# A planned mixer kernel: whole loads, low-rank matrices loaded earlier, halved weight casts, and ring space in the plan's queue model

## The chip, the cores and the metric

One core of one Trainium2 chip. The metric is the device time of one execution in microseconds (us). The kernel before takes 176.11 us (median of three runs, 175.78 to 177.19).

## The reference

A gated linear recurrence over 4 batches of 8 heads, 768 steps and 48 features, then a mixer: a low-rank mix along the sequence (U is 768 x 32, V is 32 x 768), and a two-layer MLP along the model dimension (384 to 1536 to 384, relu) with residuals.

```python
for t in range(S):
    state = alpha[:, :, t, :, None] * state + np.einsum('bhd,bhe->bhde', k[:, :, t], v[:, :, t])
    y[:, :, t] = np.einsum('bhd,bhde->bhe', q[:, :, t], state)
x = y.transpose(0, 2, 1, 3).reshape(B, S, H * D)
u = x + (x.transpose(0, 2, 1) @ U @ V).transpose(0, 2, 1)
out = u + np.maximum(u @ w_ch1, 0.0) @ w_ch2
```

## The kernel before

The kernel is written as a list of operations, each with an engine, an assumed cost, what it reads and writes, and a priority. When the kernel is built, a small planner (`Plan.run`) simulates the engines with these costs and fixes **the order of the instructions on every engine**. On the chip each engine takes its instructions in that fixed order and waits on semaphores. So an assumed cost takes no time itself.

All transfers go through one queue, SyncE's. Its model in the planner:

```python
if eng == "SP":
    clock[eng] = max(t + op.hold, dma)          # an issue waits for the transfers before it
    dma = max(dma, t + 1200.0) + op.cost        # a load is given 4400 ns
    op.end = dma + 1700.0                       # data there 1700 ns later
```

The loads of a batch, those of the last one in pieces of 4, 2, 3 and 8 heads:

```python
cuts = (4, 2, 3, 8)
def pieces(t, src, n):
    w = cuts[n] if b in (3,) else H
    for h0 in range(0, H, w):
        h1 = min(h0 + w, H)
        nc.sync.dma_start(t()[:, h0 * NC : h1 * NC, 0:D], src[b, h0:h1].rearrange("h (c p) d -> p (h c) d", p=C))
for n, (t, src) in enumerate(zip(ts, (alpha, k, q, v))):
    P.add("SP", 4400, lambda t=t, src=src, n=n: pieces(t, src, n), w=[t], prio=b + n / 10)
```

For each group of two chunks of 128 steps (three groups a batch), the kernel makes rk and rq (k and q times the decay factors) and rv (v cast to bf16), transposes rk and rq into kt and qt (by TensorE in batches 0 and 1, by the DMA in batches 2 and 3), multiplies them to scores, masks these (pm), and forms the state and y. Then come the low-rank mix (utx, xb), its transposed form uT, and the MLP. The sizes of buffers and the engine of each copy are tables. Where TensorE has nothing to do early on, the planner inserts filler products, meant to keep its clock up.

Of the kernel before, what the change touches and what calls it, by code (L numbers as in the profile page):

```python
# [48 lines left out]

class Op:  # L50
    __slots__ = ("eng", "cost", "fn", "prio", "deps", "bufs", "n", "end", "users", "est", "i", "hold")


class Plan:
# [12 lines left out]
    def add(self, eng, cost, fn, r=(), w=(), prio=0.0, after=(), kind=None, hold=450.0):  # L67
        op = Op()
        op.eng, op.cost, op.fn, op.prio = eng, cost, fn, prio
        op.i, op.hold = len(self.ops), hold  # L70
        op.deps, op.users, op.est, op.end = set(), [], 0.0, None
        for k in r:
            d = self.writer.get(k)
            if d is not None:
                op.deps.add(d)
        for k in w:
            d = self.writer.get(k)
            if d is not None:
                op.deps.add(d)
            op.deps.update(self.readers.get(k, ()))  # L80
        for k in r:
            self.readers.setdefault(k, []).append(op)
        for k in w:
            self.writer[k] = op
            self.readers[k] = []
        op.deps.update(x for x in after if x is not None)
        if kind is not None:
            if kind in self.kinds:
                op.deps.add(self.kinds[kind])
            self.kinds[kind] = op  # L90
        op.deps.discard(op)
        op.bufs = []
        for k in list(r) + list(w):
            b = k[0] if isinstance(k, tuple) else k
            if isinstance(b, Buf) and b not in op.bufs:
                op.bufs.append(b)
        for b in op.bufs:
            b.left += 1
        self.ops.append(op)
        return op  # L100

    def run(self):
# [10 lines left out]
        dma = 0.0  # L113
        fill = self.fill[0]
        todo = len(self.ops)
        while todo:
# [42 lines left out]
            if eng == "SP":  # L159
                clock[eng] = max(t + op.hold, dma)  # L160
                dma = max(dma, t + 1200.0) + op.cost
                op.end = dma + 1700.0
            else:
                clock[eng] = t + op.cost
                op.end = t + op.cost
# [26 lines left out]
def kernel(  # L192
# [12 lines left out]
    nc = tc.nc  # L205
# [39 lines left out]
    rk_s = slots("rk", 3, [C, G, H, 64], BF16)  # L245
# [11 lines left out]
    pms = Pool(slots("pm", 5, [C, 2, HP, C], BF16))  # L257
# [36 lines left out]
    def load_low_rank():  # L294
        UE, VE = ("DVE","POOL")
# [8 lines left out]
        P.add("SP", 500, lambda: nc.sync.dma_start(u_in(), moe_U.rearrange("(c p) r -> p c r", p=128)), w=[(t, 4)], prio=0.3)  # L304
        for g in range(4):
            P.add("SP", 400, lambda g=g: nc.sync.dma_start(vm_in()[32 * g : 32 * g + R, :], moe_V), w=[(t, g)], prio=0.3)
# [3 lines left out]
    def load_big():  # L310
# [4 lines left out]
        engs = ["POOL"]*6  # L315
        cost = {"ACT": 1480, "POOL": 1470}
        for i, (src, dst) in enumerate(parts):
# [7 lines left out]
            P.add("SP", 2000, lambda src=src, stage=stage: nc.sync.dma_start(stage(), src), w=[(t, i)], prio=0.5 if i < 3 else 1.35)  # L325
            P.add(engs[i], cost[engs[i]], lambda dst=dst, stage=stage, e=engs[i]: copy(e, dst, stage()), r=[(t, i)], w=[("w1" if i < 3 else "w2", i % 3)], prio=400 + i)
# [6 lines left out]
    dbank = [gen,gen3,gen3,gen3]  # L333

    def load(b):
        ts = [Buf(io) for _ in range(4)]
        cuts = (4, 2, 3, 8)

        def pieces(t, src, n):
            w = cuts[n] if b in (3,) else H  # L340
            for h0 in range(0, H, w):
                h1 = min(h0 + w, H)
                nc.sync.dma_start(t()[:, h0 * NC : h1 * NC, 0:D], src[b, h0:h1].rearrange("h (c p) d -> p (h c) d", p=C))  # L343

        for n, (t, src) in enumerate(zip(ts, (alpha, k, q, v))):
            P.add("SP", 4400, lambda t=t, src=src, n=n: pieces(t, src, n), w=[t], prio=b + n / 10)
        return ts

    def stage_gla(b, g, sprev, xb, ins):
# [8 lines left out]
        ek = ("POOL", "POOL", "DVE")[g] if first else "POOL"  # L358
        ekt = ("DVE", "DVE", "ACT")[g] if first else "ACT"
        pe = 900 + g if first else pr + 2  # L360
        eq = ("POOL", "DVE", "DVE")[g] if first else ("DVE" if b in (0,1) else "POOL")
        ev = ("POOL", "DVE", "DVE")[g] if first else "POOL"
        eqt = ("ACT", "DVE", "ACT")[g] if first else ("ACT" if b in () else "DVE")
# [4 lines left out]
        def ch(t):  # L368
            return t().rearrange("p (h c) w -> p c h w", c=NC)[:, c0 : c0 + G, :, 0:D]

        lt = Buf(lts)
        P.add("ACT", 850, lambda: nc.scalar.activation(lt()[:, :, :, 0:D], ch(at), AF.Ln), r=[at], w=[lt], prio=890 if first else pr + 4)  # L372
        rv = Buf(rvs)
        P.add(ev, ccpy[ev], lambda: copy(ev, rv(), ch(vt)), r=[vt], w=[rv], prio=pr + 3)
# [25 lines left out]
        def f_mul(eng, dst, src, fac):  # L400
            ENG[eng].tensor_tensor(dst()[:, :, :, 0:D], ch(src), fac().rearrange("t g (h d) -> t g h d", d=D), op=ALU.mult)  # L401

        P.add(ek, cmul[ek], lambda: f_mul(ek, rk, kt, ai), r=[kt, ai], w=[rk], prio=pr + 2)
        P.add(eq, cmul[eq], lambda: f_mul(eq, rq, qt, aa), r=[qt, aa], w=[rq], prio=pr + 2)

        def f_tr(src, tb):
            t = bf(tb()).rearrange("p (e c) -> p e c", c=C)
            for i in range(G):
# [8 lines left out]
        for src, dst, eng, cost in ((rk, kT, ekt, 1015 if ekt == "ACT" else 640), (rq, qT, eqt, 1015 if eqt == "ACT" else 640)):  # L417
            if b in (2,3):
                P.add("SP", 1000, lambda src=src, dst=dst: nc.sync.dma_start_transpose(dst().rearrange("p g e c -> p (g e) c"), src().rearrange("t g h w -> t (g h w)")), r=[src], w=[dst], prio=pr / 1000 - 1, hold=1250.0)  # L419
                continue  # L420
            tb = Buf(gen)
            P.add("PE", mm(*[C] * 8), lambda src=src, tb=tb: f_tr(src, tb), r=[src], w=[tb], prio=pr + 2, after=[done.get(kk - win)])
            P.add(eng, cost, lambda dst=dst, tb=tb, eng=eng: copy(eng, dst().rearrange("p g e c -> p (g e c)"), bf(tb())), r=[tb], w=[dst], prio=pr + 1)

        pm = []
        for i in range(G):
# [16 lines left out]
            P.add("PE", mm(*[C] * 4) * 1.2, f_sc, r=[kT, qT], w=[sc], prio=pr + 1, after=[done.get(kk - win)])  # L443
# [39 lines left out]
        dops[kk] = P.add("PE", mm(*[D] * 8) if final else mm(*[2 * D] * 8, *[D] * 8), f_d, r=[rk, rv], w=[db], prio=pr + 1, after=[dops.get(kk - 1), done.get(kk - 1)])  # L483
# [11 lines left out]
        em = ("ACT", "ACT", "DVE")[g] if first else "ACT"  # L495
# [25 lines left out]
        for i in range(G):  # L521
            ys.append(P.add("PE", 240, lambda i=i: f_y(i, False), r=[pm[i], rv], w=[(yb, i, 0)], prio=pr + 0.5, after=[dops[kk]]))
            sin = (sprev, 1) if i == 0 else (st, 0)
            if sin[0] is not None:
                ys.append(P.add("PE", 210, lambda i=i: f_y(i, True), r=[qT, sin], w=[(yb, i, 1)], prio=pr, after=[dops[kk]]))
# [7 lines left out]
        if b < 1 and c0 + G == NC:  # L533
# [7 lines left out]
    def stage_mix(b, xb, uT):  # L541
# [12 lines left out]
        if b < 1:  # L554
# [5 lines left out]
        P.add("ACT", 490, lambda: nc.scalar.copy(utx(), xu()[:, 0, 0:DM]), r=[(xu, 0)], w=[utx], prio=pr)  # L560
        if b == 0:
            P.fill_end = op
        if b in (0,):
            for hf in range(2):
                for j in range(NCT):
# [7 lines left out]
                    P.add("PE", mm(TW), lambda hf=hf, j=j, tb=tb: nc.tensor.matmul(tb()[:, 0, 0:TW], lhsT=utx()[:, j * C : (j + 1) * C], rhs=vm_sb[:, hf * TW : (hf + 1) * TW], start=False, stop=True, skip_group_check=True), r=[utx, "vm"], w=[tb], prio=pr)  # L573
# [3 lines left out]
        for c in range(NC):  # L577
            hb = Buf(mlp)
            P.add("PE", mm(DM), lambda c=c, hb=hb: nc.tensor.matmul(hb()[:, 0, 0:DM], lhsT=vm_sb[:, c * C : (c + 1) * C], rhs=utx(), start=True, stop=True), r=[utx, "vm"], w=[hb], prio=pr + 1)  # L579
            P.add("DVE", 550, lambda c=c, hb=hb: nc.vector.tensor_tensor(xb()[:, c, :], xb()[:, c, :], hb()[:, 0, 0:DM], op=ALU.add), r=[hb, (xb, c)], w=[(xb, c)], prio=pr)  # L580
            if b in (2,3):
                if c % 3 == 2:
                    P.add("SP", 1100, lambda c=c: nc.sync.dma_start_transpose(uT()[:, c - 2 : c + 1].rearrange("p c j t -> p (c j) t"), xb()[:, c - 2 : c + 1, :].rearrange("p c m -> p (c m)")), r=[(xb, c - i) for i in range(3)], w=[(uT, c // 3, j) for j in range(NCT)], prio=pr / 1000 - 1, hold=1300.0)
# [19 lines left out]
    def mlp1(b, uT, h1, tt):  # L603
        for jt in range(NJ):
# [13 lines left out]
            for cts in ([(0,), (1,), (2,)] if b in (0,) and jt < 2 else [(0, 1, 2)]):  # L618
                P.add("PE", mm(*[TW] * len(cts)), lambda f=f, cts=cts: f(cts), r=[n for n in need if len(n) < 3 or n[2] in cts] + [("w1", jt // 4)], w=[hb], prio=pr)
# [5 lines left out]
    def mlp2(b, xb, h1, c, utx):  # L625
        hb = Buf(mlps[b])
        pr = 5000 + b * 1000 + 100 + (c % 3) * 33 + (0 if c < 3 else 100)
        for g in range(NJ // 1):
# [8 lines left out]
            P.add("PE", mm(*[DM] * 1), f, r=[(h1, jt) for jt in range(1 * g, 1 * (g + 1))] + [("w2", g * 1 // 4)], w=[hb], prio=pr + g)  # L637
        if utx is not None:
            P.add("PE", mm(DM), lambda: nc.tensor.matmul(hb()[:, 0, 0:DM], lhsT=vm_sb[:, c * C : (c + 1) * C], rhs=utx(), start=False, stop=True), r=[utx], w=[hb], prio=pr + 9)
        ou = Buf(outs)  # L640
        P.add("DVE", 550, lambda: nc.vector.tensor_tensor(ou(), xb()[:, c, :], hb()[:, 0, 0:DM], op=ALU.add), r=[hb, (xb, c)], w=[ou], prio=100)  # L641
        P.add("SP", 550, lambda: nc.sync.dma_start(out[b, c * C : (c + 1) * C, :], ou()), r=[ou], prio=-1)
# [48 lines left out]
```

## Time and profile before

| quantity | before |
|---|---|
| median | 176.11 us |
| span of the profiled run, mean granted clock | 174.7 us, 0.990 |
| PE (TensorE) busy | 160.1 us, 92% |
| filler products within that | 16.8 us |
| first product of the MLP | 32.04 us |
| DMA packets, of them under 512 B | 63394, 37520 |
| the chain that ended last | PE 43%, DMA 24%, the queue of SyncE (SPq) 18% |

SyncE issues the transfers one after the other; as I read the traces, an issue lasts until there is room for it (0.7 us where it passes at once). The timeline of that queue gives start, duration, line, what is transferred.

```profile
11.73 4.00 SPq L343 DMA_DIRECT2D io<-in_v_dram  x1
15.78 4.45 SPq L304 DMA_DIRECT2D io<-in_moe_U_dram  x1
20.28 1.93 SPq L306 DMA_DIRECT2D io<-in_moe_V_dram  x4
```

The small U (98 kB) is issued at 15.78 us and holds the queue for 4.45 us. It has little to transfer, so what it waits for is, as I read it, v in front of it (v landed at 21.6 us).

### The profile page before, as it was taken

To read this page: it belongs to the slowest core of one execution; us is meant where nothing else is said; L and a number is where in the kernel's file an instruction comes from. 1 tells how busy PE (TensorE), PEld (TensorE's weight loads), DVE (VectorE), ACT (ScalarE), POOL (GpSimd) and SP (SyncE) were. 2 spreads that over 40 slices of the span, in tenths; PEclk is the share of its full clock that TensorE was granted. 3 is DMA by queue.
4 is the path that set the end of the run, shared out by engine and by line. 5 is a ranking of instruction groups with operands and counts; after the bars stand their busy time and mean duration, and the time that the engine had idled before them with its cause. 6 is when DMAs were issued, how large, how long until landed. Compare 5 with 4: busy or idle time off the path is not lost.

```text
span 174.7 us, 4027 instructions
## 1 busy us (share of the span) xinstructions
PE 160.1 (92%) x1696; PEld 103.0 (59%) x1696; DVE 89.9 (51%) x144; ACT 77.7 (44%) x136; POOL 53.0 (30%) x49
## 2 busy tenths in 40 slices
PE   5998798999889899989999999299999999999992
PEld 4876576666566476555665655156666566666660
DVE  1005893553695425375855738036775584543421
ACT  2284486668914391774435285205513410523200
POOL 4007378503365803796000037393000000000000
PEclk9999999999999999999999999969999999999999
DMA  3889989899989699799899989599500119101122
GB/s 94 254 246 270 258 257 388 247 269 272 266 283 378 193 276 267 228 282 200 187 245 195 238 215 256 131 201 241 120 33 16 49 50 220 45 0 49 51 85 90
DMA packets 63394, 33.39 MB, mean 191 GB/s; under 512 B 37520, under 2 KB 62096, under 8 KB 63376
## 3 DMA queue, kind: packets, MB, share of 16 engines
q1 hardware_dynamic: 63376, 33.13, 71.1%
q8 instruction: 13, 0.21, 0.5%
q14 instruction: 5, 0.04, 0.1%
HBM read 24.08 MB, written 4.72 MB: 165 GB/s over the span
## 4 chain that ended last, share of the span: by engine, by line
PE 43%; DMA 24%; SPq 18%; POOL 6%; DVE 4%; ACT 2%; issue 2%; ACTq 0%; POOLq 0%
PE ps L632 19%; PE ps L610 15%; SPq L343 12%; DMA io<-in_v_dram 9%; DMA io<-in_k_dram 6%; DMA io<-in_moe_w_ch_dram 5%; DMA io<-in_alpha_dram 4%; SPq L325 3%; SPq L419 3%; POOL rk L401 2%; PE ps L436 2%; POOL rv L292 2%; PE ps L410 1%; DVE rq L401 1%; PE ps L515 1%
## 5 line engine op out<-in xcount | busy, mean ns | idle before, releaser
L632 PE MATMUL ps<-w_sb,h1t 128*128 128x384 bf16 x288 | 57.1, 332 | 0.5 <-POOL w_sb L292 0.5
L610 PE MATMUL ps<-uT,w_sb 128*128 128x384 bf16 x288 | 52.8, 328 | 0.0
L621 ACT ACTIVATE h1t<-ps 128x384 bf16<-128x384 f32 x48 | 23.5, 490 | 44.4 <-PE ps L610 44.2
L623 DVE TENSOR_SCALAR h1t<-ps 128x384 bf16<-128x384 f32 x48 | 26.6, 556 | 24.4 <-PE ps L610 22.0
L632 PEld LDWEIGHTS <-h1t 128*128 128x128 bf16 x288 | 27.2, 99 | 18.6 <-issue 1.9
L610 PEld LDWEIGHTS <-w_sb 128*128 128x128 bf16 x288 | 27.5, 99 | 18.1 <-issue 0.8
L401 POOL TENSOR_TENSOR rk<-io,ai 128x768 bf16<-128x768 f32 x11 | 18.8, 1711 | 45.8 <-ACT ai L394 30.9
L446 DVE TENSOR_TENSOR pm<-ps,ut_ones 128x1024 bf16<-128x1024 f32 x21 | 25.4, 1221 | 8.9 <-PE ps L436 8.6
L641 DVE TENSOR_TENSOR ou<-xb,ps 128x384 f32<-128x384 bf16 x24 | 13.3, 552 | 15.7 <-PE ps L632 12.8
L645 PE MATMUL ps<-ones,ident 128*128 128x256 bf16 x122 | 16.8, 290 | 1.9 <-POOL ident masks.py:199 1.9
L531 ACT CAST xb<-ps 128x768 bf16<-128x768 f32 (+1 forms) x13 | 9.7, 749 | 12.3 <-PE ps L515 11.0
L645 PEld LDWEIGHTS <-ident 128*128 128x128 bf16 x122 | 12.2, 104 | 4.5 <-POOL ident masks.py:199 1.9
L372 ACT ACTIVATE lt<-io 128x768 bf16<-128x768 f32 x12 | 10.1, 850 | 8.3 <-DMA io<-in_alpha_dram 7.7
L401 POOL TENSOR_TENSOR rq<-io,aa 128x768 bf16<-128x768 f32 x7 | 11.5, 1641 | 4.9 <-DMA io<-in_q_dram 4.9
L292 POOL CAST rv<-io 128x768 bf16<-128x768 f32 x10 | 8.0, 824 | 10.7 <-DMA io<-in_v_dram 7.0
L580 DVE TENSOR_TENSOR xb<-xb,ps 128x384 bf16<-128x384 bf16 x18 | 9.5, 551 | 2.9 <-PE ps L579 2.6
L394 ACT ACTIVATE ai<-ps 128x768 bf16<-128x768 f32 x12 | 9.8, 819 | 2.1 <-PE ps L381 2.1
L436 PE MATMUL ps<-qt,kt 48*128 48x128 bf16 x192 | 9.2, 218 | 0.9 <-ACT xb L531 0.5
L395 ACT ACTIVATE aa<-ps 128x768 bf16<-128x768 f32 x12 | 9.9, 825 | 0.0
L292 POOL CAST w_sb<-io 128x1536 bf16<-128x1536 f32 x6 | 8.8, 1465 | 3.0 <-DMA io<-in_moe_w_ch_dram 3.0
L515 PEld LDWEIGHTS <-pm 128*128 128x128 bf16 x192 | 7.5, 96 | 2.8 <-issue 0.3
L515 PE MATMUL ps<-rv,pm 128*128 128x48 bf16 x192 | 8.4, 184 | 0.3 <-DVE pm L446 0.3
(63 smaller groups left out, 125.4 us busy)
## 6 DMA issues: line engine op xcount, KB each, us to landing
io<-in_moe_w_ch_dram SPq DMA_DIRECT2D x6, 768.0 KB, 7.7
out_dram<-ou SPq DMA_DIRECT2D x24, 192.0 KB, 2.3
io<-in_alpha_dram SPq DMA_DIRECT2D x2, 576.0 KB, 5.8
io<-in_k_dram SPq DMA_DIRECT2D x4, 288.0 KB, 4.3
io<-in_q_dram SPq DMA_DIRECT2D x2, 432.0 KB, 5.5
io<-in_moe_V_dram SPq DMA_DIRECT2D x4, 96.0 KB, 2.3
io<-in_q_dram SPq DMA_DIRECT2D x1, 288.0 KB, 6.0
io<-in_moe_U_dram SPq DMA_DIRECT2D x1, 96.0 KB, 6.3
```

The lines of the kernel that those rows point to most:

```text
L292: ENG[eng].tensor_copy(dst, src)
L343: nc.sync.dma_start(t()[:, h0 * NC : h1 * NC, 0:D], src[b, h0:h1].rearrange("h (c p) d -> p (h c) d", p=C))
L401: ENG[eng].tensor_tensor(dst()[:, :, :, 0:D], ch(src), fac().rearrange("t g (h d) -> t g h d", d=D), op=ALU.mult)
L436: nc.tensor.matmul(s2[:, par, p, :], lhsT=kT()[o : o + D, i, p, :], rhs=qT()[o : o + D, i, p, :], start=(p == 0), stop=(p == HP - 1),)
L446: nc.vector.tensor_tensor(pmi().rearrange("t two hp c -> t (two hp) c"), sc().rearrange("p two (hp c) -> p (two hp) c", c=C), maskc.to_bro ...
L515: nc.tensor.matmul(y2[:, par, p, :], lhsT=pm[i]()[:, par, p, :], rhs=rv()[:, i, 2 * p + par, :], start=s0, stop=s1, skip_group_check=True,)
L610: nc.tensor.matmul(hb()[:, 0, 0:TW], lhsT=w1_sb[:, ct, jt * 128 : (jt + 1) * 128], rhs=uT()[:, 3 * tt : 3 * tt + 3, ct, :], start=(ct == 0 ...
L621: P.add("ACT", 500, lambda jt=jt, hb=hb: nc.scalar.activation(h1()[:, jt, :], hb()[:, 0, 0:TW], AF.Relu), r=[hb], w=[(h1, jt)], prio=100)
L623: P.add("DVE", 560, lambda jt=jt, hb=hb: nc.vector.tensor_scalar_max(h1()[:, jt, :], hb()[:, 0, 0:TW], 0.0), r=[hb], w=[(h1, jt)], prio=100)
L632: nc.tensor.matmul(hb()[:, 0, 0:DM], lhsT=h1()[:, jt, (c % 3) * C : (c % 3 + 1) * C], rhs=w2_sb[:, jt, :], start=(jt == 0), stop=(jt == NJ ...
L641: P.add("DVE", 550, lambda: nc.vector.tensor_tensor(ou(), xb()[:, c, :], hb()[:, 0, 0:DM], op=ALU.add), r=[hb, (xb, c)], w=[ou], prio=100)
L645: P.fill_fn = lambda i: nc.tensor.matmul(ps[:, i, 0:256], lhsT=ident, rhs=fill_in, start=True, stop=True)
```

## The change

Its intent: load every batch whole, bring U and V in earlier (U between alpha and k, V between q and v), shorten the copies on the way to the first product of the MLP, cast the weights in halves, so that products can start after half a cast, and give the planner a queue model with 512 ring places, in which a load takes 385 places and a small transfer 40.

```diff
             if eng == "SP":
-                clock[eng] = max(t + op.hold, dma)
-                dma = max(dma, t + 1200.0) + op.cost
-                op.end = dma + 1700.0
+                free = t
+                for s, f, n in ring:
+                    x = sum(m for s2, f2, m in ring if s2 >= s) + op.descs - RING
+                    if x > 0:
+                        free = max(free, s + (f - s) * min(1.0, x / n))
+                clock[eng] = free + op.hold
+                s = max(dma, clock[eng] + 850.0)
+                dma = s + op.cost
+                ring.append((s, dma, op.descs))
+                del ring[:-24]
+                op.end = dma + op.land                 # land: 550 ns
 # low rank: U, then V
-        UE, VE = ("DVE","POOL")
+        UE, VE = ("DVE","DVE")
-        P.add("SP", 500, ... moe_U ..., prio=0.3)
+        P.add("SP", 400, ... moe_U ..., prio=0.05)
-            P.add("SP", 400, ... moe_V ..., prio=0.3)
+            P.add("SP", 300, ... moe_V ..., prio=0.205)
 # weights: each cast in two halves, those of w2 shared by POOL and ACT
-            P.add(engs[i], cost[engs[i]], ... copy(e, dst, stage()) ...)
+            for hf in range(2):
+                e = ((("POOL","POOL"),)+(("POOL","POOL"),)*2+(("POOL","ACT"),)*3)[i][hf]
+                ...
 # loads
-            P.add("SP", 4400, ... pieces(t, src, n), w=[t], prio=b + n / 10)
+            P.add("SP", 4100, ... src[b] whole ..., prio=b + n / 10, hold=800.0, descs=385)
 # engines, first batch (three groups) and others
-        ek = ("POOL", "POOL", "DVE")[g] if first else "POOL"
+        ek = ("DVE", "POOL", "DVE")[g] if first else "POOL"
-        eq = ("POOL", "DVE", "DVE")[g] if first else ("DVE" if b in (0,1) else "POOL")
+        eq = ("POOL", "DVE", "DVE+POOL")[g] if first else ("DVE" if b in (0,) else "POOL")
 # ... likewise for rv, kt, qt, st; rk 3 -> 4 buffers, pm 5 -> 4, any PSUM bank for the state;
# state product of a group allowed earlier; last group's y and its low-rank product in two steps in batches 1 and 2 too;
 # the evacuation of utx in batch 0 is split between DVE and ACT
```

The `...` stand for cuts. The arithmetic is the same.

## The prediction

> **What bounds the kernel now.** I read the page's slices first, to see which resource is full when; then the same quantities in short stretches around the one visible hole; then the queue's own order of time, to see what the hole waited for; then the DMA counts of single stretches, to see what a load costs in each form.
>
> The slices (4.37 us each):
>
> ```profile
> PE   5998798999889899989999999299999999999992
> PEclk9999999999999999999999999969999999999999
> DMA  3889989899989699799899989599500119101122
> ```
>
> Three stretches can be seen. Up to slice 28 (about 124 us) the DMA row is nearly full. PE is full too, but its first 32 us are mostly filler (L645, 16.8 us of PE's 160.1): the first product of the MLP (L610) starts at 32.04 us. From about 113 us on PE works without a gap until 171.3 us, while DMA is almost idle. Between them lies slice 25 with PE at 2, and slice 26 with the granted clock at 6. In stretches of 2 us:
>
> ```profile
> 106.00:108.00 2.00, 2.00 (x14) 1.21 (x13) 1.90 (x5) 0.53 (x1) 2.00 (x2) 1.00 1.03 298
> 108.00:110.00 2.00, 1.51 (x10) 0.79 (x8) 0.57 (x2) 1.36 (x2) 0.00 (x0) 1.00 0.62 175
> 110.00:112.00 2.00, 0.00 (x0) 0.00 (x0) 0.00 (x0) 0.15 (x1) 0.00 (x0) 1.00 0.36 117
> 112.00:114.00 2.00, 1.01 (x20) 0.78 (x20) 0.42 (x2) 0.03 (x1) 1.89 (x2) 1.00 0.92 198
> 114.00:116.00 2.00, 2.00 (x9) 0.95 (x7) 0.40 (x1) 0.28 (x1) 2.00 (x3) 0.58 1.07 243
> 116.00:118.00 2.00, 2.00 (x8) 1.01 (x7) 0.56 (x1) 0.13 (x1) 2.00 (x2) 0.56 1.83 153
> ```
>
> The columns are PE, PEld, DVE, ACT and POOL busy, the clock, DMA share and GB/s. PE stands from 109.5 to 113.0 us (0.02 us busy in 3.5), and then runs about 4 us at a clock of 0.57: 4 x 0.43 = 1.7 us more. The hole costs 3.5 + 1.7 = 5.2 us. Why it stands, from the queue in order of time:
>
> ```profile
> 85.53 2.86 SPq L343 DMA_DIRECT2D io<-in_alpha_dram  x2
> 88.44 7.07 SPq L343 DMA_DIRECT2D io<-in_k_dram  x4
> 95.62 5.83 SPq L343 DMA_DIRECT2D io<-in_q_dram  x3
> 101.97 0.99 SPq L642 DMA_DIRECT2D out_dram<-ou  x2
> 103.17 0.74 SPq L343 DMA_DIRECT2D io<-in_v_dram  x1
> 104.01 6.60 SPq L642 DMA_DIRECT2D out_dram<-ou  x1
> 110.72 1.27 SPq L419 DMA_TRANSPOSE kt<-rk  x1
> 112.09 1.25 SPq L583 DMA_TRANSPOSE uT<-xb  x1
> ```
>
> v of the last batch lands at 103.17 + 8.8 = 112.0 us (the chain has it as 8.80 us of DMA), POOL casts it, PE goes on at 112.99. The other supply of work, the transposed u of batch 2 (uT), was ready for transposing at 105.9 and 108.6 us (ends of the xb additions on DVE), but the in-order queue stood 6.6 us on one store in front of it; L610 resumes only at 116.67. So the late loads of batch 3 set the end: 112 us plus 59 us of unbroken PE work. Why are they late? The same counts for a stretch with whole loads (24 to 44 us) and one with loads in pieces (84 to 100 us), in that order:
>
> ```profile
> DMA packets 5873, 5.93 MB, mean 297 GB/s; under 512 B 96, under 2 KB 4738, under 8 KB 5870
> ```
>
> ```profile
> DMA packets 17322, 3.46 MB, mean 216 GB/s; under 512 B 17320, under 2 KB 17320, under 8 KB 17320
> ```
>
> 5.93 MB / 5873 is 1.0 kB a packet; 3.46 MB / 17322 is 200 B, that is one 48-float row. The pieces cut by heads lose the joining of rows into packets. In finer slices whole loads hold some 315 to 320 GB/s, pieces some 250.
>
> **What the Trainium skill says.** "DMA: Bandwidth & Descriptors", section "Why small descriptors are slow (HBM only)": each packet carries a fixed overhead on the engine's internal bus, which joining successive descriptors spreads. The trace agrees: 200 B packets at about 250 GB/s against 320. "TensorE: Matmul & The Clock Gate", section "Part 1: The HAM clock gate": after an idle window of about 3.4 us the clock halves, and a busy window brings it back. Here 3.5 us of idleness are followed by about 4 us at 0.56 to 0.58, which agrees; so filling the hole brings back both costs, and even shortening it may bring back the second. The first page's section "Queues, rings and completion order" says that descriptors on each engine are taken in ring order. Its consequence here is my reading of the queue: the 6.6 us block contains 3.6 us of waiting for an output (DVE ends it at 107.65) and then 3 us in which nothing is left but lack of queue space behind v.
>
> **The change part by part.**
>
> Whole loads for batch 3: alpha, k and q were 2, 4 and 3 pieces, 9 issues become 3. Landings: batch 1, whole, at 35.9, 39.9, 44.4, 49.3 us (issue plus time to landing), 4.1 to 4.9 apart; batch 2 alpha, k, q at 60.8, 65.4, 70.4, 4.6 to 5.0 apart. Batch 3 in pieces: alpha at 93.3, q at 104.7, 5.7 a load. At 4.7 a load, three loads give 3 x 1.0 = 3.0 us; by rates, 1.18 MB / 250 - 1.18 MB / 319 = 1.0 us each, the same. v then lands at about 109.0 and the queue is free about 3 us earlier, at 107.6, so that uT's transposes go out as soon as their data is there. PE ran dry at 109.5. With v's cast (0.82 us) and the semaphores, 0.3 to 0.5 us of the hole remains, too short for the clock. Gain 3.0 of the 3.5 us, and the 1.7 us of clock: 4.7 us on the path.
>
> Ring space in the plan: no instruction of its own. The queue's order changes; a store no longer counts as if it waited for the whole load before it. It may clear other holes (DMA share 0.60 at 58 to 60, 0.57 at 72 to 74 us), but PE is 95% busy there. Against it: old costs (4.4 us a load, 1.7 to landing) put the first four landings within 0.5 us of the trace, the new ones (4.1, 0.55) some 0.5 us early for alpha and 2 us early for v, so engines that take instructions in order may be planned onto data that is not there. I take 0.5 us loss for it.
>
> Weight casts in halves: six POOL casts of 1.465 us become twelve of some 0.75; for w2 one of each two goes to ACT. The last part landed at 56.78, PE waited 0.46 us for its cast until 58.3, and POOL's rk behind it ran 58.26 to 60.68, for which PE waited 0.27 us. Halves give back up to 0.7 us; I take 0.5. ACT has room (1.43 us busy of 5 at 50 to 55).
>
> U and V ahead: U (98 kB) before k, V (4 x 98 kB) before v. The total before w1 stays, so only k, q (about 0.5 us later) and v (about 1.7 us later, 21.6 to 23.3) move. rk went to DVE (1.10 against 1.65 us), which covers k's delay; POOL loses vm's cast (0.82 us between two masks it alone does) to DVE. v was wanted at 23.59 us by PE, now at about 24.1. I count 0.3 us loss at the start.
>
> Evacuation by two engines: one ACT copy of 0.478 us becomes 0.35 beside another, 0.13 us gained once, on the path to 32.04. rq of batch 1 moves from DVE (0.9 us alone) to POOL (1.64), with DVE busy with masks then: zero.
>
> Sum: -4.7 + 0.5 - 0.5 + 0.3 - 0.1 = -4.5 us. 176.1 - 4.5 = 171.6; that other holes of PE between 45 and 109 us (1.0, 0.7, 0.5 and 0.5 us of idleness, 3 us of filler) shrink a little by the better order takes 0.4: 171.2 us.
>
> **The rivals.** First, the whole gain of 5.2 + 0.7 us with holes cleared: the bound is PE, whose work after 113 us is full in every stretch. 168 us. For it: batch 3's loads could start before 85.5 us, since the queue waited 4.5 us for an output before. Against it: DMA is 0.9 and more busy from 80 to 100 us, with transposes at some 200 GB/s. Second, the hole moves: the new order sends stores or transposes before v, or an optimistic plan sets PE behind a load: 2 to 4 us come back, 174 to 176 us. The tight margin (v at 109.0, PE dry at 109.5) speaks for it; the plan's explicit ring against. Third, the start: v's 1.7 us falls in full on the first batch, everything shifts by up to 1.5 us: 172.7. Against it: batch 1's loads, not batch 0, hold PE at 45 to 50 us, and their place in the stream is unchanged.
>
> **Range and chances.** 168 and 175 are the first and second rival; PE-bound work makes less than 167.5 hardly possible. The 2% line is 172.6, above my figure by 1.4 us, roughly the size of the second rival's smaller half. Faster 0.68, same 0.29, slower 0.03: no part removes overlap worth 3.5 us.
>
> **What would show it.** Right: packets under 512 B fall from 37520 to about 20000; the three loads of batch 3 land 4.3 to 5.0 us apart; no PE slice below 7 between 32 us and the end; PEclk 9 throughout; L610 of the MLP starts within 0.7 us of 32.0; waits for w_sb gone. Wrong: a new stall over 3.4 us with a clock dip, v of batch 3 after 111 us, or a start after 33 us.

## The result

The changed kernel takes **182.03 us** (median of four runs, 181.34 to 183.14), against 176.20 us for the kernel before in the same rounds (175.78 to 177.19). The ratio is 1.033, with a 95% interval of 1.025 to 1.040: slower. Ratios in this document are the mean time of one kernel's runs over that of the other's of the same rounds, so not quite the ratio of the medians quoted. Executions over 1.5% slower than the fastest of the same kernel are left out of the means. The prediction of 171.2 us had the wrong direction.

The slices of the changed kernel's page (40 slices of 4.49 us, in tenths):

```profile
PE   5999597999998999955899999599999999999992
PEclk9999999699999999999699999999999999999999
DMA  4898799788979798699797998399601128101122
```

In slice 25 PE is up from 2 to 5, and the clock no longer dips after it. But slices 17 and 18 (76 to 85 us) are at 5, slice 19 has a new dip, and there is another dip in slice 7 (31 to 36 us). Packets under 512 B fell from 37520 to 18992, as predicted.

To see where time is lost, and not only where PE stands, I count **work done by a time t**: per 5 us, PE's busy time without filler products, times the granted clock, summed up. Both kernels have about 141.6 us of it. The difference of two kernels at t says how many us of work one is behind. It is my sum, from the busy times, filler times and clocks of the windows, and is as good as their busy times: in the runs further below the sum comes to 139.5 to 141.8 us, though all make the same products, so "behind" is good to about 1 us, and in bw_tab (139.5) to about 2:

| by t (us) | 25 | 35 | 50 | 60 | 75 | 80 | 85 | 90 | 110 | 115 | 120 | end |
|---|---|---|---|---|---|---|---|---|---|---|---|---|
| work done, before | 6.7 | 16.1 | 28.8 | 37.3 | 52.0 | 56.0 | 60.9 | 65.9 | 84.9 | 86.8 | 90.4 | |
| changed kernel behind by | 1.1 | 5.0 | 2.7 | 2.2 | 2.0 | 3.6 | 6.0 | 8.3 | 7.4 | 6.3 | 5.0 | 5.0 |

The last number is the difference of the spans (179.7 - 174.7). So there are three places. The start loses 5.0 us. About half of that comes back by 60 us, since both kernels then wait for batch 1's loads. The stretch from 75 to 90 us loses 6.3 us. At the old hole, from 110 to 120 us, 2.4 us come back.

### The new hole at 75 to 90 us

In stretches of 5 us (PE, PEld, DVE, ACT, POOL busy, granted clock, DMA share, GB/s), first the kernel before, then the changed one:

```profile
75.00:80.00 5.00, 4.54 (x37) 2.84 (x37) 3.06 (x7) 3.57 (x6) 4.89 (x5) 1.00 1.02 303
80.00:85.00 5.00, 4.95 (x70) 2.96 (x69) 3.20 (x6) 2.03 (x5) 1.52 (x2) 1.00 1.09 190
85.00:90.00 5.00, 5.00 (x77) 3.29 (x76) 2.84 (x6) 2.03 (x4) 0.00 (x0) 1.00 0.98 204
```

```profile
75.00:80.00 5.00, 3.75 (x27) 2.01 (x25) 3.09 (x6) 2.93 (x5) 3.52 (x4) 1.00 0.92 282
80.00:85.00 5.00, 2.58 (x49) 1.78 (x48) 1.18 (x3) 2.63 (x5) 3.68 (x4) 1.00 1.11 147
85.00:90.00 5.00, 4.08 (x35) 1.99 (x36) 0.87 (x2) 0.81 (x2) 0.00 (x0) 0.66 0.77 203
```

Busy times are down to 2.58 us, and then the clock is 0.66. What PE stood for, from the timeline of PE in the changed kernel (in brackets the idle time before the row, and its releaser):

```profile
80.60 0.48 PE L499 MATMUL ps<-rv,rk 128*64 128x96 bf16 x16 [1.80 <-POOL rv L304]
...
82.53 0.65 PE L643 MATMUL ps<-uT,w_sb 128*128 128x384 bf16 x3
85.92 0.34 PE L541 MATMUL ps<-st,qt 48*128 48x48 bf16 x8 [2.74 <-DMA qt<-rq]
```

PE first waits for rv, then for the transposed qt. Only three products of the MLP (L643) stand between. In the kernel before, 15 such products stand at the same place and nine more a little later, with no wait in front of the product of state and qt:

```profile
77.66 2.60 PE L610 MATMUL ps<-uT,w_sb 128*128 128x384 bf16 x15
...
80.60 1.64 PE L610 MATMUL ps<-uT,w_sb 128*128 128x384 bf16 x9
82.29 0.27 PE L510 MATMUL ps<-st,qt 48*128 48x48 bf16 x8
```

Why both inputs came late can be read from POOL's timeline. First before, then after:

```profile
77.41 1.64 POOL L401 TENSOR_TENSOR rq<-io,aa 128x768 bf16<-128x768 f32 x1
79.16 2.36 POOL L292 CAST rv<-io 128x768 bf16<-128x768 f32 x3
```

```profile
76.60 1.64 POOL L427 TENSOR_TENSOR rk<-io,ai 128x768 bf16<-128x768 f32 x1
79.72 1.59 POOL L304 CAST rv<-io 128x768 bf16<-128x768 f32 x2 [1.48 <-DMA io<-in_v_dram]
81.27 1.64 POOL L427 TENSOR_TENSOR rq<-io,aa 128x768 bf16<-128x768 f32 x1
```

Before, POOL makes all of rk and rq and takes the casts of v last, when v has just landed (79.1 us). In the changed kernel two casts of v stand **in front of** the last rq. v lands at 79.6 us, POOL stands 1.48 us, and rq and its transpose follow late. The planner thought v would be there: its own landing time for this load was 70.4 us. (0.87 us is added to the planner's times here, so that both begin with the first issue at the same time.) Its beliefs against the trace:

| landing, us | v, batch 0 | alpha 1 | v 1 | alpha 2 | v 2 | alpha 3 | v 3 |
|---|---|---|---|---|---|---|---|
| before: plan / trace | 21.4 / 21.6 | 36.2 / 35.9 | 49.4 / 49.3 | 59.8 / 60.8 | 77.7 / 79.1 | 90.1 / 93.3 | 105.1 / 112.0 |
| after: plan / trace | 22.4 / 24.3 | 32.8 / 36.1 | 46.0 / 51.3 | 56.4 / 62.7 | 70.4 / 79.6 | 80.7 / 93.9 | 95.6 / 111.5 |

The old model is within 1.4 us up to batch 2. The new one is early by 1.9 us at first, 9.2 us at v of batch 2 and 15.9 us at the end.

### The old hole at 110 us

It shrank, but v of the last batch lands at 111.5 us where 109.0 had been predicted. The queue of the changed kernel:

```profile
87.06 0.72 SPq L362 DMA_DIRECT2D io<-in_alpha_dram  x1
87.89 5.40 SPq L448 DMA_TRANSPOSE kt<-rk  x1
93.38 1.25 SPq L448 DMA_TRANSPOSE qt<-rq  x1
95.10 0.71 SPq L362 DMA_DIRECT2D io<-in_k_dram  x1
```

A transpose now stands behind alpha and holds the queue 5.40 us; before, all of these transposes were out ahead of alpha. In the ring model it would fit beside the load (385 + 66 places of 512) and pass at once. So k is issued at 95.10 instead of 88.44 us, and the 3 us that whole loads save are gone before v is issued.

### The start

The queue of the changed kernel:

```profile
11.49 6.33 SPq L318 DMA_DIRECT2D io<-in_moe_V_dram  x4
18.02 0.71 SPq L362 DMA_DIRECT2D io<-in_v_dram  x1
```

V's four small transfers hold the queue for 6.33 us. The first waits 4.93 us of it, as U did before, behind a load. v's issue begins at 18.02 us (before 11.73) and ends at 18.73 us (before 15.73, since there v itself waited 4.00 us at this place), and v lands at 24.3 us (before 21.6). So what the four transfers cost v is some 3 us, not 6. U, in front of k, costs even less: k's issue ends at 6.73 us instead of 6.53, since k now passes in 0.72 us. While V and v waited in the queue, the DMA engines ran dry: their share is 0.66 from 15 to 20 us, where it was 0.94. PE in the changed kernel:

```profile
29.97 0.25 PE L541 MATMUL ps<-st,qt 48*128 48x48 bf16 x6
31.39 0.23 PE L541 MATMUL ps<-st,qt 48*128 48x48 bf16 x2 [1.17 <-issue]
...
36.20 2.11 PE L643 MATMUL ps<-uT,w_sb 128*128 128x384 bf16 x12
```

The first product of the MLP comes at 36.20 us, 4.2 us later than before. On the way there the last mask of batch 0 on POOL ends at 30.49 us (before 28.09), because two half casts of w1 were planned in front of it, and the clock is 0.66 from 30 to 35 us.

### The profile page after: what moved, and what is told of

The parts are those of the page before. It is cut to its first block, busy times and chain, and to the rows that moved or that the text cites. A ratio compares the mean times of both kernels' runs of the same rounds, so it can differ in the third digit from the quotient of the medians.

```text
span 179.7 us, 4030 instructions
## 1 busy us (share of the span) xinstructions
PE 162.9 (91%) x1699; PEld 104.0 (58%) x1699; DVE 90.7 (50%) x147; ACT 78.3 (44%) x139; POOL 54.1 (30%) x53
## 2 busy tenths in 40 slices
DMA packets 49474, 33.39 MB, mean 186 GB/s; under 512 B 18992, under 2 KB 48176, under 8 KB 49456
## 4 chain that ended last, share of the span: by engine, by line
PE 38%; SPq 36%; DMA 16%; issue 3%; POOL 3%; DVE 1%; ACT 0%; POOLq 0%; DVEq 0%; ACTq 0%
SPq L362 19%; PE ps L665 18%; PE ps L643 14%; DMA io<-in_v_dram 10%; SPq L336 7%; DMA io<-in_alpha_dram 6%; SPq L448 5%; SPq L318 3%; SPq L316 2%; PE ps L467 1%; POOL rv L304 1%; POOL rk L427 1%; POOL rq L427 1%; PE ps L612 1%; SPq L675 1%
## 5 line engine op out<-in xcount | busy, mean ns | idle before, releaser
L665 PE MATMUL ps<-w_sb,h1t 128*128 128x384 bf16 x288 | 55.4, 326 | 0.7 <-POOL w_sb L304 0.7
L643 PE MATMUL ps<-uT,w_sb 128*128 128x384 bf16 x288 | 54.7, 332 | 0.1
L643 PEld LDWEIGHTS <-w_sb 128*128 128x128 bf16 x288 | 27.4, 99 | 17.8 <-issue 1.2
L427 POOL TENSOR_TENSOR rk<-io,ai 128x768 bf16<-128x768 f32 x10 | 16.7, 1670 | 26.3 <-ACT ai L420 20.2
L678 PE MATMUL ps<-ones,ident 128*128 128x256 bf16 x125 | 19.2, 308 | 1.9 <-DVE rk L259 1.9
L427 POOL TENSOR_TENSOR rq<-io,aa 128x768 bf16<-128x768 f32 x10 | 17.1, 1717 | 5.1 <-DMA io<-in_q_dram 5.0
L304 POOL CAST rv<-io 128x768 bf16<-128x768 f32 x10 | 8.4, 856 | 31.4 <-DMA io<-in_v_dram 29.4
L678 PEld LDWEIGHTS <-ident 128*128 128x128 bf16 x125 | 12.9, 110 | 5.0 <-POOL ident masks.py:199 1.9
L302 ACT CAST st<-ps 128x192 bf16<-128x192 f32 x10 | 3.2, 318 | 14.9 <-PE ps L509 8.3
L499 PE MATMUL ps<-rv,rk 128*64 128x48 bf16 (+1 forms) x160 | 5.2, 200 | 4.1 <-POOL rv L304 2.1
```

What stands on the lines that cost most here:

```text
L304: ENG[eng].tensor_copy(dst, src)
L427: ENG[eng].tensor_tensor(dst()[:, i0 : i0 + n, :, 0:D], ch(src, i0, n), fac()[:, i0 : i0 + n].rearrange("t g (h d) -> t g h d", d=D), op=A ...
L643: nc.tensor.matmul(hb()[:, 0, 0:TW], lhsT=w1_sb[:, ct, jt * 128 : (jt + 1) * 128], rhs=uT()[:, 3 * tt : 3 * tt + 3, ct, :], start=(ct == 0 ...
L665: nc.tensor.matmul(hb()[:, 0, 0:DM], lhsT=h1()[:, jt, (c % 3) * C : (c % 3 + 1) * C], rhs=w2_sb[:, jt, :], start=(jt == 0), stop=(jt == NJ ...
L678: P.fill_fn = lambda i: nc.tensor.matmul(ps[:, i, 0:256], lhsT=ident, rhs=fill_in, start=True, stop=True)
```

## The experiments

Each run was compared with the kernel before on the same chip. "Behind" is the work behind the profiled run of before, as in the table above. There were four series. In the first, second and third, before took 177.85, 176.09 and 175.54 us. In the fourth it took 178.54 us over seven runs, with only two fast ones (175.03 and 174.15 us). Identical programs differ here by 1 to 2% between series and chips, and the ratio of one and the same program came out at 0.980 and at 0.994 (before_whole and its repetition), so single effects below about 1.5% are not resolved. By the 2% rule after_latelr, bw_half2 and before_whole2 are "same" and all other verdicts of the first three series are "unclear"; the argument rests on the traces as much as on the times. Medians include the slow runs, ratios do not. The changed kernel was timed in none of these series again: where a run is set against it, two ratios to before are compared.

### First series: the parts that were suspected first

**after_oldq**: the changed kernel with the old queue model and its costs.

```diff
-                free = t
-                ...
-                op.end = dma + op.land
+                clock[eng] = max(t + op.hold, dma)
+                dma = max(dma, t + 1200.0) + op.cost
+                op.end = dma + 1700.0
-                P.add("SP", 4100, ... hold=800.0, descs=385)
+                P.add("SP", 4400, ...)
```

> The changed kernel with the plan's old queue model and its old costs (4.4 us a load, 1.7 us to landing, the queue held until the load before is through), all else of the change kept. Theory M (the new queue model believes loads early, so that PE, DVE and POOL, which take instructions in order, are lined up behind data that is not there): the hole at 78 to 90 us (6.3 us of work lost against before) goes, and the time falls from 182 to 174-178 us. Theory S (the start is delayed by U and V in front of v, and by casts in front of a mask; the plan is harmless): it stays at 180 us or more, with the first L610-type product still near 36 us.

Measured: 179.35 us, ratio 1.012 (1.004 to 1.021). Some 2% of the 3.3% go with this one part, and neither theory's range is met. It is not the whole: the start is behind by 4.6 us at 35 us, hardly less than in the changed kernel, and 2.9 us are still lost between 75 and 85 us in the profiled run (which was the slowest of the four, 181.25 us).

**before_newq**: the reverse, the kernel before with only the new queue model and its costs.

> The kernel before with the new queue model and its costs alone, nothing else changed. Theory M: slower than 176.1 by 3 to 6 us, with a hole in PE near 78 to 90 us. Theory S: within 1% of before.

Measured: 181.00 us, ratio 1.017 (1.007 to 1.027). No transfer is other than before, only the planned order (that of the queue included). It is behind by 1.1 us at 35 us, 1.8 at 75 and 8.7 at 95: the same hole, at the same place, made by the model alone. POOL's timeline has the same signature:

```profile
76.96 1.59 POOL L304 CAST rv<-io 128x768 bf16<-128x768 f32 x2 [2.62 <-DMA io<-in_v_dram]
78.52 1.64 POOL L413 TENSOR_TENSOR rk<-io,ai 128x768 bf16<-128x768 f32 x1
80.12 1.63 POOL L413 TENSOR_TENSOR rq<-io,aa 128x768 bf16<-128x768 f32 x1
```

The casts stand in front of rk and rq, and POOL waits 2.62 us for v. The model also moves a load in this run: alpha of batch 3 is issued at 77.46 us, in front of five of the transposes, where before it came behind them (85.53 us). How much of the hole is due to that, the run does not separate.

**before_whole**: the kernel before with only the pieces of batch 3 taken away. The planner's costs, and so the orders on all engines, are unchanged.

```diff
-            w = cuts[n] if b in (3,) else H
+            w = H
```

> The kernel before with the three cut loads of batch 3 issued whole, the plan (order on every engine) the same. If the prediction's step on whole loads was right: packets under 512 B fall to some 19000, v of batch 3 lands at about 109 us instead of 112, the hole at 109.5 to 113 shrinks to under 1 us, clock dip gone: 171 to 173.5 us. If loads of batch 3 are bound by something else (queue order, ring, transposes beside them): within 1% of 176.

Measured: 174.42 us, ratio 0.980 (0.970 to 0.989). Packets under 512 B are 18992, no clock dip is left, and between 110 and 120 us it moves from 1.4 us behind to 1.5 ahead. This part does what was predicted.

**after_latelr**: the changed kernel with U and V behind v again, V's cast on POOL.

```diff
-        UE, VE = ("DVE","DVE")
+        UE, VE = ("DVE","POOL")
-        ... moe_U ..., prio=0.05)
+        ... moe_U ..., prio=0.3)
-            ... moe_V ..., prio=0.205)
+            ... moe_V ..., prio=0.3)
```

> The changed kernel with U and V issued after v of the first batch and V cast on POOL, as before; all else of the change kept. Theory S: the first MLP product moves from 36.2 us back to about 32-33 us and the time falls by 2 to 5 us, to 177-180. Theory M: the start is better, but loads of batch 1 absorb it (the deficit of 5.0 us of work at 35 us had shrunk to 2.0 by 60 us), so the time moves by no more than 2 us and stays at 180-182.

Measured: 179.54 us, ratio 1.010 (1.002 to 1.017), so 2.3% better than the changed kernel, but not as expected: at 35 us it is 5.8 us behind, no better than the 5.0 of the changed kernel. The gain lies later: 4.3 us behind at 90 us instead of 8.3. At the start a new wait took the place of the old one. POOL took V's cast in front of a mask and waited 1.62 us for V to land.

### Second series: each part on top of before_whole

**bw_half**: before_whole with the half casts alone (the diff's part "weights").

> The kernel before with whole loads for batch 3 (0.98 of before on its own) plus the weight casts in halves, with w2's second halves on ACT. By the prediction (step on casts): 0.5 us faster than the whole loads alone, ratio to before near 0.977. If the halves get in front of batch 0's last mask on POOL (as the changed kernel's trace shows: two halves, 1.6 us, before a mask): 1.5 to 3 us slower than whole loads alone, ratio 0.985 to 1.0, first MLP product after 33.5 us.

Measured: 175.14 us, ratio 1.002 (0.987 to 1.017). Nothing is resolved.

**bw_b0**: before_whole with all changes to batch 0 (U and V early, engine table, utx by two engines).

> Before with whole loads plus everything that the change does to batch 0 alone: its table of engines, U between alpha and k, V before v, V cast on DVE, low-rank copy on two engines. By the prediction (0.3 us loss, 0.1 gain): ratio within 0.5% of the whole loads alone, 0.98. If this is the source of the 5 us that the changed kernel lacks at 35 us: first MLP product at 35 us or later and ratio 0.99 to 1.01.

Measured: 180.34 us, ratio 1.031 (1.020 to 1.042). It is 3.6 us behind at 35 us, with the first MLP product at 35.55 us, and it is 5.4 behind at 85. With the old queue model and whole loads, the changes to batch 0 alone come to the same ratio as the whole change. Also here V holds the queue 6.33 us (from 12.27).

**bw_gla**: before_whole with the changes to batches 1 to 3 (rq of batch 1 on POOL, any PSUM bank for the state, an earlier state product, split evacuations, four rk). pm was kept at five buffers: in this form the old model's planner finds no order with four, so that was never run.

> Before with whole loads plus the changes to batches 1 to 3: rq of batch 1 on POOL, any bank for the state products, looser order for them, last group's y copied in two parts and its low-rank product in two steps, four rk (five pm kept, since the old queue model's plan gets stuck with four). By the prediction: zero, ratio near 0.98. Rival: the trade costs in the middle, 0.985 to 1.0, with PE waiting for rq of batch 1 at 45 to 55 us.

Measured: 174.92 us, two of four runs slow (the fast ones 172.90 and 173.25 us), ratio 0.988 (0.976 to 1.000). No harm of these changes is seen; two fast runs show no more.

**after_cal**: the changed kernel with one number altered, the planned cost of a load.

```diff
-                P.add("SP", 4100, ... hold=800.0, descs=385)
+                P.add("SP", 4900, ... hold=800.0, descs=385)
```

> The changed kernel with one number changed: a load costs 4.9 us in the plan instead of 4.1, so that its landings agree with the trace within about 2 us. If the early belief is what makes the new queue model harmful, the hole at 78 to 90 us goes and the ratio to before falls from 1.033 to 1.00 or below; if the model's shape (small transfers need not wait) or the engine tables are to blame, it stays above 1.015.

Measured: 177.69 us, ratio 1.016 (1.007 to 1.024): 1.7% from a number that no instruction carries. The hole of the middle is gone: 2.5 us behind at 75 us, 2.9 at 90. POOL still has two casts of v in front of the last rq, but v has landed by then (planned 78.8 us, in the trace 78.3) and POOL does not wait:

```profile
79.70 1.60 POOL L304 CAST rv<-io 128x768 bf16<-128x768 f32 x2
```

The start (4.7 us behind at 35 us) is untouched.

### Third series: what in batch 0

**bw_lr**: before_whole with only U and V early and V's cast on DVE.

> Before with whole loads plus only the new places of U (between alpha and k) and V (in front of v), V cast on DVE. The batch-0 changes together took the ratio from 0.98 to 1.03. If the order of these small loads is the cause (the queue stands 6.3 us on V's four issues and v of batch 0 goes out at 18 instead of 12 us): nearly all of it is here, ratio 1.015 to 1.035, first MLP product at 34.5 us or later. If the table of engines is: ratio 0.975 to 0.99 here.

Measured: 179.28 us, ratio 1.026 (1.017 to 1.035), with before_whole repeated in the same series at 0.994. It is 4.8 us behind at 35 us, with the first MLP product at 36.41 us, so this alone makes a loss as large as the changed kernel's at the start. Again V waits in the queue (5.43 us), and v is issued at 19.1 and lands at 25.4 us. Between 75 and 90 us another 5.1 us are lost, with the old queue model: a late start does not just shift the rest, and the hole in this stretch is not the new model's alone. Here POOL has the casts behind the last rq, as before, and PE's waits are shorter (0.62 us for rv, 0.95 us for qt), with fillers between them.

**bw_tab**: before_whole with only the engine table and utx by two engines.

> Before with whole loads plus only the new table of engines for batch 0 and the low-rank copy on two engines; U and V stay where they were. The counterpart of the run with U and V moved: if the order of the small loads is the cause, 0.975 to 0.99 here and the first MLP product within 0.7 us of 32.0; if the table is, 1.01 or more.

Measured: 175.38 us, ratio 1.000 (0.990 to 1.009). The start is 5.9 us behind at 35 us, as bad as with U and V, yet it ends 0.3 us ahead of before: 5.2 behind at 75, 4.2 at 110, 1.1 at 115. The profiled span is 172.3 us, 2.4 us shorter than before's. The gain from 110 us on is no sign that the late start was made up there: before_whole2 (below), with the same whole loads, gains nearly as much in that stretch. Against before_whole2 the span is 1.8 us longer and the ratio 0.005 higher, which is not resolved. So here a late start shows little in the time, and in bw_lr it comes with a loss of 3%.

**bw_half2**: bw_half repeated with five rounds.

> Whole loads and half casts once more, beside the whole loads alone on the same chip, in five rounds: the first three rounds left it between 0.987 and 1.017. By the prediction (0.5 us gained) 0.975; if halves cost, over 0.985. A version that beats both kernels is looked for here.

Measured: 173.80 us, ratio 0.996 (0.988 to 1.003), beside before_whole at 0.994 in the same series. A gain of 0.5 us (0.3%) could not be seen in these runs, and none is.

**before_whole2**: before_whole repeated with five rounds.

> The kernel before with whole loads alone, once more in five rounds: 0.98 as in the first run (0.970 to 0.989). Under 0.98 with the interval clear of 1 it beats both kernels.

Measured: 174.54 us, ratio 0.994 (0.984 to 1.004), less than the 0.980 of the first series. Its profiled run, which follows the run of before within 0.7 us of work until 105 us, shows the effect clean. The windows that the prediction shows of before, here:

```profile
108.00:110.00 2.00, 0.95 (x20) 0.63 (x19) 0.00 (x0) 1.10 (x2) 1.36 (x2) 1.00 0.79 184
110.00:112.00 2.00, 2.00 (x13) 1.21 (x14) 0.82 (x2) 0.32 (x1) 2.00 (x3) 1.00 1.06 241
112.00:114.00 2.00, 2.00 (x15) 1.18 (x13) 1.11 (x2) 0.78 (x2) 2.00 (x2) 1.00 2.04 204
```

Of 3.5 us standing, 1.05 are left, and the clock stays at 1.00. v is issued at 100.75 (103.17) and lands at 108.5 us (112.0). The work goes from 0.2 us ahead at 110 us to 3.9 ahead at 120: 3.7 us gained in this stretch (the spans differ by 4.2 us).

### Fourth series: together, and apart

It was open whether U, V, the place in the queue or the planned order makes the loss.

**after_both**: the changed kernel with both undone, the old queue model and U and V late (both diffs above).

> The changed kernel with both suspects undone, the queue model (old) and the places of U and V (old, V cast on POOL); whole loads, halves, engine tables and the changes to batches 1 to 3 kept. If the two explain the loss: ratio 0.98 to 1.005 against 1.033 with both, 1.012 and 1.010 with one of them undone. If they only lead to the loss through a third part (halves, tables): 1.01 or more.

Measured: 176.11 us. Against the two fast runs of before this is 1.009 (176.09 / 174.59 by the means). It is 4.4 us behind at 35 us, 4.1 at 90 and 0.3 at the end. Undoing these two parts takes away nearly all of the loss in the profiled run, though whole loads do not then show as a gain.

**bw_u**: before_whole with only U early (`prio=0.3` to `0.05`).

> Before with whole loads plus only U between alpha and k, V left behind v. U and V together cost 3% (1.0255 against 0.994). If it is U (96 kB of 128 B rows in front of k): 1.01 or more. If it is V's four issues in front of v: 0.985 to 1.0 here.

**bw_v**: before_whole with only V early and its cast on DVE.

> Before with whole loads plus only V in front of v (cast on DVE), U left behind v: if V is the cause, 1.015 to 1.035, with v of batch 0 going out near 18 us; if U is, 0.985 to 1.0.

Measured: bw_u 176.82 us, bw_v 177.84 us (one run slow); by the means of the fast runs that is 1.014 and 1.016, but with two fast runs of before there are no verdicts. At 35 us they are 4.2 and 4.0 us behind, at the end 0.8 and 0.8 to 1.5. Either matrix alone spoils the start by as much as both, so the costs of the two don't add.

**bw_lr_act**: bw_lr with V's transfers issued from ScalarE's queue, so that they take no place in SyncE's. The plan, and so the order on the other engines, is the same.

```diff
-            ... nc.sync.dma_start(vm_in()[32 * g : 32 * g + R, :], moe_V) ...
+            ... nc.scalar.dma_start(vm_in()[32 * g : 32 * g + R, :], moe_V) ...
```

> U and V in their new places as in the run that cost 3%, the plan and so the order on PE, DVE and POOL the same, but V's four loads issued from ScalarE's queue instead of SyncE's. If the loss is v waiting in the queue behind V's issues, v goes out at 12 us again and lands near 22 us: ratio 0.99 to 1.01. If the loss is that the plan itself puts work later (rv, masks and filler ordered for a late v), it stays at 1.015 to 1.03 although v lands early.

Measured: 179.76 us, three of four runs slow, the fast one 176.78 us, so the times decide nothing. The trace, though it is of a slow run (179.92 us, clock 0.99), says more about the start:

```profile
12.30 5.08 SPq L343 DMA_DIRECT2D io<-in_v_dram  x1
```

v's issue ends at 17.38 us (in bw_lr 19.79) and v lands at 23.3 us, 2.1 earlier than in bw_lr, and yet the first MLP product comes at 36.91 us and it is 4.8 us behind at 35 us. So the loss of the start is not v's late landing alone. q did not come earlier than in bw_lr (rq starts on DVE at 19.45 us, against 19.64), and the planned order was still one for a late v (planned landing 25.8 us). V's issues now stand in ScalarE's order instead, which could cost something of its own.

**The plans themselves.** The planner of each kernel can be run without the chip. It inserts as many filler products as the trace of that kernel has (122 for before, 125 for the changed kernel, 163 for bw_lr, and likewise for all 18), so it is the plan that was built. The start of the first product of the MLP, planned (0.87 us added) and measured, in us:

| | before | changed | after_latelr | bw_tab | bw_u | after_both | after_cal | bw_b0 | bw_v | after_oldq | bw_lr | bw_lr_act |
|---|---|---|---|---|---|---|---|---|---|---|---|---|
| planned | 30.5 | 31.0 | 30.9 | 31.4 | 31.7 | 32.6 | 33.7 | 34.0 | 34.0 | 34.7 | 35.0 | 35.0 |
| measured | 32.0 | 36.2 | 36.8 | 36.5 | 35.7 | 35.3 | 35.8 | 35.6 | 37.2 | 35.5 | 36.4 | 36.9 |

So there are two kinds of late start. In bw_lr the plan itself puts the start 4.5 us later, and 4.4 us are measured; bw_b0, bw_v, after_oldq and after_cal have 3.2 to 4.2 us of it in the plan too. That also fits bw_lr_act, where v came earlier and the order did not change. In the changed kernel, after_latelr, bw_tab and bw_u the plan has at most 1.2 us of it, and the chip 3.7 to 4.7 us: there the plan was wrong about the chip. (after_both lies between, with 2.1 us planned and 3.2 measured.)

## Why the prediction was wrong, by its own steps

**Whole loads (-4.7 us): right in mechanism, smaller in size.** The packets joined, and the hole and its clock dip went. before_whole2 lands v at 108.5 us where 109.0 was predicted, leaves 1.05 us of the hole where 0.3 to 0.5 were predicted, and gains 3.7 us of work in this stretch. In time it is 2.0% in one series and 0.6% in the other, where 4.7 us would be 2.7%. In the changed kernel the gain is cut to 2.4 us, since k of batch 3 is issued 6.7 us later.

**"Ring space in the plan" (0.5 us loss): the step that failed most.** The reason against it was named in the prediction (engines in order, planned onto data that is not there), but it was sized from the first four landings, where the model is 0.5 to 2 us early. The error adds up: 1.9 us at v of batch 0, 9.2 at v of batch 2, 15.9 at the end. A model early by 9 us puts POOL's casts of v in front of rq, and takes away the MLP products that PE would have had in the meantime. It costs 1.7% alone (before_newq), and taking it away gives 2.0% (after_oldq), or 1.7% with one number set right (after_cal). That is some 3 us, against the 0.5 predicted; the hole itself takes 6.3 us of work. That the early belief makes this hole rests on before_newq and after_cal together with POOL's order; that other orders can lose as much in the same stretch, bw_lr shows (5.1 us).

**"U and V ahead" (0.3 us loss): the second.** The prediction moved only k, q and v by the bytes in front of them. v was put at 23.3 us and landed at 24.3, so that term was near, though the queue was not counted (V's issue waits behind q for 4.93 us, and v's issue behind V). What failed is the path: the loss was taken as v's delay against PE's need at 23.59 us, with the rest of the order as it was. In place of 0.3 us the first product of the MLP came 4.2 us later, and the start does not depend on v alone, as bw_lr_act suggests. Measured alone on top of whole loads, it is 1.026 against 0.994, about 3%, or some 5 us. In bw_lr the delay is in the plan (4.5 us, the table above). What exactly costs 4 to 6 us where the plan does not have it, as in the changed kernel (late q, masks behind casts, a clock at 0.66), is **not settled**: four different small changes of batch 0 (bw_u, bw_v, bw_lr, bw_tab) all give 4 to 6 us, by different waits. The order of before was good there, and each of these new ones was worse.

**Weight casts in halves (-0.5 us): not seen.** PE still waits for w_sb, 0.7 us in all against 0.5 before, and bw_half2 and before_whole2 are alike in time. Half a microsecond is below what they resolve.

**Evacuation by two engines (-0.1 us): too small to be seen.** The prediction's first sign of it, the start of the MLP within 0.7 us of 32.0, failed by 4.2 us.

**The rivals.** The second rival (the hole moves because of an optimistic plan) and the third (the start shifts) both came true, and the prediction weighed each as the alternative of the other. Their sizes were 2 to 4 and 1.5 us; the trace shows 6.3 and 5.0 us of work, of which 2.8 come back by 60 us and 2.4 at the old hole: 5.0 + 6.3 - 2.8 - 2.4 is 6.1. The remaining 1.1 us, to the 5.0 of the spans, is picked up in between (0.2 from 60 to 75 us, 0.9 from 90 to 110). The first rival, no more holes, was ruled out by the first page. Two small slips of the prediction do not matter for this: 2 to 4 us on top of 171.2 make 173 to 175, not 174 to 176, and in the two stretches with a low DMA share PE is busy 91%, not 95% (58 to 60 us: 1.65 of 2). The reason given for "slower 0.03" ("no part removes overlap worth 3.5 us") was wrong in kind. As the plan was made anew as a whole, the quality of its order was at stake too, and not only each part's own cost.

**Is there a better version?** All kernels of before_whole's family without early U or V or the new model (before_whole, bw_half2, bw_gla, bw_tab: medians 173.8 to 175.4 us) beat the changed kernel clearly. That before_whole beats the kernel before is seen in one series (0.980) and not in the next (0.994).

## What to carry to other kernels

Where instruction orders come from a simulation at build time, the simulator's costs are part of the kernel: check its believed landing times against the trace, late ones above all, since an error per load adds up, and work planned onto data that is not there stands in front of work that could run. The plan can also be asked before the chip: the plan of bw_lr foretold its late start. Count for each transfer when its issue ends, not when it begins: a small transfer behind a large one waited 4.0 to 4.9 us in the changed kernel, but a load at that place had waited too, so the load behind it lost 0.2 us (k behind U) or 3 us (v behind V). Change such a plan one part at a time: the parts here, whose costs had been summed singly, did not add.

## What the Trainium skill lacked or had wrong

- "DMA: Bandwidth & Descriptors", section "Queues, rings and completion order", describes rings and their order, but does not say when an issue is held up. Here U (98 kB), issued right behind alpha in the changed kernel, held the queue for 4.01 us, and V behind q for 4.93 us. With alpha's transfer taken as some 2.4 to 7.2 us (first bytes to landing), and q's as 12.8 to 18.2 (k's landing to q's), that is, by this estimate, until about seven tenths and two thirds of the load in front were through. The plan's 512 places, into which a small transfer fits beside a load, are not borne out.
- The same page, section "Issuing engines are not separate DMA queues", says that starting transfers on several engines saves only the time on the sequencer, which is usually small beside the transfer. Here V on ScalarE's queue let v's issue end at 17.38 instead of 19.79 us, and v landed 2.1 us earlier: some 2 us, which is not small beside the 4 to 5 us between two loads, but the first product of the MLP came no earlier for it.
- The same page, section "Why small descriptors are slow (HBM only)", gives every packet a fixed overhead. The runs agree: with 18992 packets under 512 B instead of 37520, v of the last batch landed 3.5 us earlier (before_whole2).
- "TensorE: Matmul & The Clock Gate", section "Part 1: The HAM clock gate", ties the fall of the clock to an idle window of about 3.4 us. In the changed kernel the clock is 0.66 from 30 to 35 us, where the longest single gap is 1.17 us, among short products and fillers (PE busy 0.85 us from 29 to 30, 0.22 from 30 to 31, then the clock at 0.50 from 32 to 34). So a window that is only partly idle can be enough here. The same page tells further down of short idle times that make the clock go up and down, without a length; how much is enough, no run here shows either.
